# The first query and key rows in four-token packets: one transfer per head pair, 64x64 transposes, order of issue fitted anew

## The chip, the cores and the metric

The kernel runs on one core of one Trainium2 chip. The metric is device microseconds of one execution, as the median of three runs: 359.04 before the change (358.71 to 359.33). One execution was recorded by the hardware profiler; all views of the profile come from it. The engines are TensorE (PE for its products, PEld for its weight loads), VectorE (DVE), ScalarE (ACT), GpSimd (POOL) and SyncE (SP). SP and ACT issue transfers on hardware queues; POOL issues the transfers that also convert from float32 to bfloat16, on a software queue. All queues share 16 DMA engines.

## The reference

The reference has two stages. The first is attention in a sliding window with sinks: each query sees the first four keys and the 128 last ones up to itself. Its output, 3072 tokens of 512 numbers, goes into a mixture of four experts, all of them used for every token and weighted by normalized probabilities.

```python
# q, k, v: (4, 8, 768, 64); n_sink 4, window 128
scores = np.matmul(q, k.transpose(0, 1, 3, 2)) / np.sqrt(D)
keep = (pos[None, :] < n_sink) | ((rel >= 0) & (rel < window))   # rel = query - key position
scores = np.where(keep, scores, -1e9)
a = softmax(scores)                      # in the reference by exp, sum and division
x = (a @ v).transpose(0, 2, 1, 3).reshape(3072, 512)

p = domain_probs / domain_probs.sum(-1, keepdims=True)           # (3072, 4)
out = 0                                  # w1: (4, 512, 1024), w2: (4, 1024, 512)
for e in range(4):
    out += p[:, e:e + 1] * (np.maximum(x @ w1[e], 0) @ w2[e])
```

## The kernel before

The tokens of a batch (768) are worked in three groups of 256, `g` = 0, 1, 2; the 8 heads in four pairs, `hp` = 0 to 3. Two heads of 64 numbers fill the 128 partitions. For each group of a batch, attention needs query and key with the head's numbers on the partitions (tile `qkT`). In batch 0 they are turned by TensorE (`transposes`, tile `tr`); in the later batches by transposing transfers. Then come, pair by pair, the score products (`scores`, tile `sps`), the exponential on ScalarE (tile `aT`), a product with the mask on VectorE, the value products (`values`, tile `od`; a column of ones in `vx` gives the sum of the softmax), the division on VectorE or ScalarE (tile `onat`), and the turn into `xT`, which the experts read. In group 0 of batch 0 the mask is a bias that TensorE adds to the scores (`low`, with the identity as the stationary operand), so nothing is multiplied there.

The experts' first layer (`emit_first`, tile `hps`, line 1106) is a plain product for the first groups. Later it is done by seven products in place of eight on quarters of the matrices (`emit_fast`, tile `cps`, line 1189), whose operands VectorE forms from weights and tokens (`weight_form1`, `tokens`). The second layer is plain for two groups (`emit_second`, line 1433) and by seven products after that (`emit_product`, line 1358).

The first query and key rows, 256 tokens of 8 heads, are loaded as float32 by `load_first`, before anything else: queries on SP's queue, keys on ACT's, in two transfers each, one for heads 0 to 3 and one for heads 4 to 7. A partition holds two neighbouring tokens of each head, 512 bytes at a stretch. `cast_first` converts each half to bfloat16, queries on VectorE and keys on ScalarE. Then four transposes of 128x128 turn a head pair (line 595): two token phases for queries, two for keys, both heads at once. The copy to `qkT` puts the tokens back into their order. The rows of groups 1 and 2 are loaded by POOL with the conversion on the way (`load_nat`), and turned as 128x64 pieces (line 598).

The order of all instructions is made while the program is built. A loop at the end of the kernel keeps an estimated clock for each engine and for the transfers (the dictionary `t`, the functions `pe`, `act`, `dve`, `pool`, `lands`), asks which steps are ready (`options`, `firsts`, `product_ready`, `second_ready`), and emits the best by a rank. Work for VectorE and ScalarE is put on a list with a due time (`later`) and emitted in the order of these (`flush`). The named constants at the head of the kernel are ranks, due times, waiting times and shares of this planner. They do not change what is computed, but what stands before what on each engine; on the chip each engine then takes its instructions strictly in that order. While nothing is ready in the first 20 us of the plan, the loop emits products on zeros (`idle_products`, line 574), whose results nobody reads. Nine of them with 512 columns stand at the very start.

Of the kernel before, what the change touches and what calls it, by code (L numbers as in the profile page):

```python
# [16 lines left out]
def kernel(  # L17
# [42 lines left out]
    NGATE = 5  # L60
    START = {0: (1, 0), 1: (0, 1), 2: (0, 0), 3: (0, 0)}
# [3 lines left out]
    SHARE_OF = (0.634, 1.111, 1.102)  # L65
    LEAD = (1.272, 0.235)
    DUE = 0
    LOW_PRODUCT = 2.791
    LOW_SECOND = 4.402
    HIGH_PRODUCT = 0.207  # L70
    EARLY = 0.154
    GATE = 8921
    GATE0 = 5401
    FORM = 20576
    FORM2 = 37391
    TOKEN00 = 33179
    TOKEN0 = 1119
    WAIT2 = 16164
    WAIT1 = 5898
    LATE3 = 3  # L80
    TOKEN = 11155
    MARGIN = 494
    FULL = 7
    STEP0 = 0.141
    READY = 46
    WIDE = 2
    OPEN = 1.198
# [6 lines left out]
    GROW = 24662  # L94
    ONLY2 = 1
    BEHIND = 7198
# [14 lines left out]
    FLIP = 421  # L111
# [175 lines left out]
    def load_first():  # L287

        raw = {name: mo.tile([P, 2, 4, 2 * D], FP32, name=f"{name}raw", tag=f"wide{i}", bufs=1) for i, name in enumerate("qk")}
        for half in range(2):  # L290
            hs = slice(4 * half, 4 * half + 4)
            for name, src in (("q", q), ("k", k)):
                x = raw[name][:, half]
                (nc.sync if name == "q" else nc.scalar).dma_start(
                    out=x, in_=src[0, hs, 0:G, :].rearrange("h (p t) d -> p h (t d)", t=2),
                )
                nat[0, half, name, "raw"] = x
            landed["first", half] = ((4870.0, 5180.0), (7550.0, 7350.0))[half]
            t["sp"] += 530
# [4 lines left out]
    first = {name: sb.tile([P, 2, H, D], BF16, name="qkn", tag="qkn", bufs=NQB) for name in "qk"}  # L304
# [3 lines left out]
    def cast_first(half):  # L308
        hs = slice(4 * half, 4 * half + 4)

        def cast(at):
            cast_at[half] = at

        part = join(2, cast)
        for i, name in enumerate("qk"):
            def run(engine, i=i, name=name):
                copy(
                    engine, first[name][:, :, hs, :],
                    nat[0, half, name, "raw"].rearrange("p h (t d) -> p t h d", t=2),
                )  # L320
                part(clock(engine, 512))
            later(("dve", "act")[i], landed["first", half][i], 0, run)
# [215 lines left out]
    low = [lent[:, 5 * P:8 * P], lent[:, 8 * P:10 * P]]  # L538
# [1066 lines left out]
```

## Time and profile before

| What | Before |
|---|---|
| Median of 3 runs | 359.04 us (358.71 to 359.33) |
| The profiled execution | 358.95 us, of which its span is 357.2 us |
| TensorE products | 348.8 us busy, 98% of the span |
| VectorE | 306.7 us, 86% |
| ScalarE | 168.7 us, 47% |
| GpSimd | 70.5 us, 20% |
| First transfers of q and k issued | from 0.81 us |
| First product, on zeros | at 1.40 us |
| First transposes of group 0 and of group 1 | at 5.83 and 13.00 us |
| First product of an expert | at 15.10 us |

The span goes from the first to the last recorded instruction; the execution's own time is 1.75 us longer than its span. A group of instructions is named by the line, the engine, the operation, and what it writes and reads. A product counts as busy from its first column to the modelled end of its results, so neighbouring products overlap, and the distance from one start to the next is what a product takes away from the next one: 0.11 us for 256 columns and 0.43 us for the 512 columns of the first products. A DMA is shown by its issue on the issuing engine and by the time from there to its landing. The granted clock of TensorE is 1.00 in all slices.

### The profile page before, as it was taken

The numbers are of one execution on the slowest core, as the hardware profiler recorded it, in microseconds if no ns is written. First come the engines' busy times: TensorE is split into PE (matmuls) and PEld (weight loads), VectorE is DVE, ScalarE is ACT, GpSimd is POOL, SyncE is SP. The second block draws the span as 40 slices with busy tenths as digits, with TensorE's granted clock in tenths as the row PEclk, the third lists the DMA queues.
The fourth block names the chain that finished last, engine by engine and source line by source line (L and its number), as shares of the span: only waits on it lengthen the run. The fifth ranks groups of instructions, "written<-read, shape, count | busy, mean of one in ns | idle before, by whom it ended". The sixth has DMA issues, their size and how long they took to land.

```text
span 357.2 us, 11108 instructions
## 1 busy us (share of the span) xinstructions
PE 348.8 (98%) x4673; PEld 302.6 (85%) x4673; DVE 306.7 (86%) x701; ACT 168.7 (47%) x432; POOL 70.5 (20%) x90
## 2 busy tenths in 40 slices
PE   8999999999999999999999999999999999999995
PEld 3675687777688998998998998899899999999884
DVE  6669999998799899899699799699799699999630
ACT  5866451437882922566444722926443632322110
POOL 8934114311260440420030620000000000000000
PEclk9999999999999999999999999999999999999999
DMA  9999999999993999691086999124112221100011
GB/s 175 185 195 203 230 210 174 137 135 139 227 148 42 138 168 157 75 119 46 32 68 111 148 156 139 50 54 55 44 32 63 59 52 51 37 31 31 1 61 60
DMA packets 115318, 37.86 MB, mean 106 GB/s; under 512 B 97196, under 2 KB 110764, under 8 KB 115268
## 3 DMA queue, kind: packets, MB, share of 16 engines
q0 software_dynamic: 74416, 17.31, 55.4%
q1 hardware_dynamic: 39796, 19.32, 29.3%
q8 instruction: 36, 0.59, 0.7%
q10 hardware_dynamic: 1056, 0.52, 0.6%
q14 instruction: 14, 0.11, 0.1%
HBM read 41.03 MB, written 6.34 MB: 133 GB/s over the span
## 4 chain that ended last, share of the span: by engine, by line
PE 83%; DVE 6%; ACT 5%; DMA 2%; issue 1%; POOL 1%; DVEq 0%
PE cps L1189 35%; PE acc L1358 31%; PE acc L1433 7%; PE hps L1106 3%; PE sps L706 3%; ACT onat L825 2%; PE od L786 2%; ACT aT L746 2%; DMA vx<-in_v_dram 2%; DVE H L1223 1%; DVE cps L1239 1%; DMA gates<-gate_rows 1%; PE od L779 1%; DVE onat L816 1%; DVE H L1254 1%
## 5 line engine op out<-in xcount | busy, mean ns | idle before, releaser
L1189 PEld LDWEIGHTS <-w 128*128 128x128 bf16 x1408 | 87.1, 98 | 3.5 <-issue 1.0
L1358 PEld LDWEIGHTS <-H 128*128 128x128 bf16 x720 | 66.6, 98 | 7.9 <-issue 1.2
L1223 DVE SCALAR_TENSOR_TENSOR H<-cps,gates 128x512 bf16<-128x512 f32 x105 | 69.8, 683 | 0.0
L1358 PE MATMUL acc<-w,H 128*128 128x256 bf16 x432 | 56.8, 273 | 0.1
L1189 PE MATMUL cps<-xT,w 128*128 128x128 bf16 x704 | 52.5, 219 | 0.5 <-ACT onat L825 0.5
L1189 PE MATMUL cps<-T,w 128*128 128x128 bf16 x704 | 52.5, 219 | 0.1
L746 ACT ACTIVATE aT<-sps 128x512 bf16<-128x512 f32 (+1 forms) x96 | 46.5, 571 | 9.7 <-PE sps L706 9.5
L1232 ACT COPY cps<-cps 128x512 f32<-128x512 f32 x44 | 25.7, 592 | 44.2 <-PE cps L1189 33.8
L1405 ACT COPY osb<-acc 128x256 f32<-128x256 f32 x40 | 15.4, 384 | 59.2 <-PE acc L1358 59.2
L825 ACT ACTIVATE onat<-od,R 128x64 bf16<-128x64 f32 x144 | 32.8, 349 | 21.7 <-DVE R L813 21.7
L1358 PE MATMUL acc<-wf,H 128*128 128x256 bf16 x288 | 39.3, 273 | 0.0
L1189 PEld LDWEIGHTS <-qkn 128*128 128x128 bf16 x576 | 34.8, 98 | 1.1 <-issue 0.2
L1239 DVE TENSOR_TENSOR cps<-H,cps 128x512 f32<-128x512 f32 x40 | 27.7, 691 | 9.0 <-PE cps L1189 6.2
L1358 PEld LDWEIGHTS <-S 128*128 128x128 bf16 x320 | 30.2, 98 | 4.2 <-issue 1.0
L1245 ACT COPY H<-cps 128x512 f32<-128x512 f32 x40 | 23.7, 600 | 18.1 <-PE cps L1189 18.1
L1433 PE MATMUL acc<-w,H 128*128 128x512 bf16 x128 | 30.1, 379 | 0.0
L1189 PEld LDWEIGHTS <-vf 128*128 128x128 bf16 x480 | 28.8, 98 | 0.1
L331 POOL DMA_DIRECT2D vx<-in_v_dram x24 | 21.4, 909 | 37.4 <-PE od L786 25.9
L1254 DVE TENSOR_TENSOR H<-H,cps 128x512 f32<-128x512 f32 x40 | 27.0, 680 | 1.7 <-PE cps L1189 1.6
L271 POOL DMA_DIRECT2D rows<-in_q_dram x18 | 16.0, 887 | 61.1 <-DMA qkT<-rows 51.0
L1189 PE MATMUL cps<-T,qkn 128*128 128x128 bf16 x384 | 27.3, 219 | 0.1
L727 DVE TENSOR_TENSOR aT<-aT,mask 128x1024 bf16<-128x1024 bf16 (+1 forms) x36 | 22.8, 641 | 1.9 <-ACT aT L746 1.6
(123 smaller groups left out, 524.2 us busy)
## 6 DMA issues: line engine op xcount, KB each, us to landing
w<-in_moe_w_dram POOLq DMA_DIRECT2D x7, 1024.0 KB, 23.1
out_dram<-osb SPq DMA_DIRECT2D x23, 256.0 KB
gates<-gate_rows SPq DMA_DIRECT2D x40, 128.0 KB
vx<-in_v_dram POOLq DMA_DIRECT2D x24, 128.0 KB, 10.0
rows<-in_q_dram POOLq DMA_DIRECT2D x18, 128.0 KB, 6.4
rows<-in_k_dram POOLq DMA_DIRECT2D x18, 128.0 KB, 6.7
w<-in_moe_w_dram POOLq DMA_DIRECT2D x4, 256.0 KB, 8.4
kraw<-in_k_dram ACTq DMA_DIRECT2D x2, 256.0 KB
```

Source lines behind the costliest of these rows:

```text
L331: nc.gpsimd.dma_start(out=vx[tb][:, :, 0:D], in_=v[b, :, tb * P:(tb + 1) * P, :].rearrange("h p d -> p h d"),)
L727: nc.vector.tensor_mul(x, x, m[:, None, :].to_broadcast([P, n, 2 * w // n]))
L746: nc.scalar.activation(out=a[:, ph], in_=sps[ph][:, 0:w], func=AF.Exp, scale=scale)
L825: nc.scalar.mul(o[:, qi, hp, ph * D:(ph + 1) * D], od[:, qi, ph, 0:D], R[:, qi, ph])
L1189: nc.tensor.matmul(y[:, f], lhsT=A[:, d, f * P:(f + 1) * P], rhs=T[:, d], start=(m in ("P1", "P5") and f == 0 and d == 0), stop=(d == 1), ...
L1223: nc.vector.scalar_tensor_tensor(out=dst, in0=src, scalar=0.0, in1=gate, op0=ALU.max, op1=ALU.mult)
L1232: nc.scalar.copy(out=tiles["Y"], in_=y)
L1239: nc.vector.tensor_add(tiles["V"], c5, tiles["X"])
L1245: nc.scalar.copy(out=c5, in_=y)
L1254: nc.vector.tensor_add(c5, c5, y)
L1358: nc.tensor.matmul(x, lhsT=self.operand(b, g, e, m)[:, f], rhs=forms[e][m][:, f], start=(k == 0 and f == 0 and m in (("P1", "P5", "P2") if ...
L1433: nc.tensor.matmul(op, lhsT=H[:, fb // QF, fb % QF, s], rhs=w2_sb[e][:, fb, :], start=(fb == 0), stop=(fb == NFB - 1),)
```

## The change

The first query and key rows are loaded in another layout. There are now eight transfers, one per head pair for queries and one for keys. Head `a` of a pair takes 64 partitions, and each partition holds four neighbouring tokens of one head, 1024 bytes at a stretch. All queries and the keys of the last pair are on SP's queue, the keys of the first three pairs on ACT's. The conversion follows per pair: the first pair's both on VectorE, later ones queries on VectorE and keys on ScalarE.

A pair is then turned by sixteen transposes of 64x64 instead of four of 128x128: for queries and keys, four token phases for each head, where a head reads and writes its own 64 partitions. The copies to `qkT` put four phases back in order instead of two.

The second bias tile, which nothing read but the second mask, is gone from ScalarE; the second mask is made by two instructions of VectorE from the running maximum (`own`). The clearing of small tiles and the making of the masks are now put on VectorE's list with due times, so that they stand behind the conversion of the second pair's queries and ahead of the third's. Nine idle products with 512 columns at the start become five. Most constants of the planner have new values. In the resulting order VectorE converts the first pair and the second pair's queries, makes the small tiles and the masks, converts the third pair's queries, and only then copies the first turned pair; TensorE turns three pairs, scores three pairs, turns the fourth, and takes the values of two pairs, then of the third, then scores the fourth pair. Seventeen idle products with 256 columns stand in the order instead of twelve. POOL issues the key rows of group 2 before the products for the sink keys and values instead of behind them. From group 1 on, the order on all engines is the old one up to places where neighbours are swapped, in about seven stretches on TensorE and a dozen on VectorE.

```diff
@@ -58,42 +58,49 @@
     NGATE = 5
+    RUN = 4
+    FIRST = (3350.0, 4050.0, 4750.0, 5450.0)
+    CAST = (("dve", "dve"), ("dve", "act"), ("dve", "act"), ("dve", "act"))
+    BEGIN = (3450.0, 3600.0)
+    CLEAR = 1000
+    NACT = 3
+    NIDLE = 5
...
-    SHARE_OF = (0.634, 1.111, 1.102)
-    LEAD = (1.272, 0.235)
+    SHARE_OF = (0.61, 1.111, 1.102)
+    LEAD = (1.272, 0.328)
...
-    GATE = 8921
-    GATE0 = 5401
-    FORM = 20576
-    FORM2 = 37391
-    TOKEN00 = 33179
+    GATE = 9087
+    GATE0 = 5108
+    FORM = 22227
+    FORM2 = 45355
+    TOKEN00 = 35179
...
-    FLIP = 421
+    FLIP = 80
...
@@ -286,40 +293,35 @@
 
     def load_first():
 
-        raw = {name: mo.tile([P, 2, 4, 2 * D], FP32, name=f"{name}raw", tag=f"wide{i}", bufs=1) for i, name in enumerate("qk")}
-        for half in range(2):
-            hs = slice(4 * half, 4 * half + 4)
+        raw = {name: mo.tile([P, NHP, RUN * D], FP32, name=f"{name}raw", tag=f"wide{i}", bufs=1) for i, name in enumerate("qk")}
+        for hp in range(NHP):
             for name, src in (("q", q), ("k", k)):
-                x = raw[name][:, half]
-                (nc.sync if name == "q" else nc.scalar).dma_start(
-                    out=x, in_=src[0, hs, 0:G, :].rearrange("h (p t) d -> p h (t d)", t=2),
+                x = raw[name][:, hp]
+                (nc.scalar if name == "k" and hp < NACT else nc.sync).dma_start(
+                    out=x,
+                    in_=src[0, 2 * hp:2 * hp + 2, 0:G, :].rearrange("h (p t) d -> h p (t d)", t=RUN),
                 )
-                nat[0, half, name, "raw"] = x
-            landed["first", half] = ((4870.0, 5180.0), (7550.0, 7350.0))[half]
+                nat[0, hp, name, "raw"] = x
             t["sp"] += 530
 
     def copy(engine, out, in_):
         (nc.scalar.copy if engine == "act" else nc.vector.tensor_copy)(out=out, in_=in_)
 
-    first = {name: sb.tile([P, 2, H, D], BF16, name="qkn", tag="qkn", bufs=NQB) for name in "qk"}
+    first = {name: sb.tile([P, NHP, RUN, D], BF16, name="qkn", tag="qkn", bufs=NQB) for name in "qk"}
     qkn_free[-2:] = [1e12] * 2
     cast_at = {}
 
-    def cast_first(half):
-        hs = slice(4 * half, 4 * half + 4)
+    def cast_first(hp):
 
         def cast(at):
-            cast_at[half] = at
+            cast_at[hp] = at
 
         part = join(2, cast)
         for i, name in enumerate("qk"):
-            def run(engine, i=i, name=name):
-                copy(
-                    engine, first[name][:, :, hs, :],
-                    nat[0, half, name, "raw"].rearrange("p h (t d) -> p t h d", t=2),
-                )
-                part(clock(engine, 512))
-            later(("dve", "act")[i], landed["first", half][i], 0, run)
+            def run(engine, name=name):
+                copy(engine, first[name][:, hp].rearrange("p t d -> p (t d)"), nat[0, hp, name, "raw"])
+                part(clock(engine, 256))
+            later(CAST[hp][i], FIRST[hp], 100 * hp, run)
 
     def rows_at(b, g):
         return max(landed.get(("qk", b, tb), 1e12) for tb in (2 * g, 2 * g + 1))
@@ -535,36 +537,40 @@
     nc.vector.tensor_tensor_scan(own, ident, ident, 0.0, ALU.add, ALU.max)
     two = own[:, None, :].to_broadcast([P, 2, P])
     LOW = 32768.0
-    low = [lent[:, 5 * P:8 * P], lent[:, 8 * P:10 * P]]
+    low = lent[:, 5 * P:8 * P]
     nc.vector.tensor_scalar(
-        out=low[0].rearrange("p (n q) -> p n q", n=3)[:, 0::2], in0=two, scalar1=LOW, scalar2=-LOW, op0=ALU.mult, op1=ALU.add,
+        out=low.rearrange("p (n q) -> p n q", n=3)[:, 0::2], in0=two, scalar1=LOW, scalar2=-LOW, op0=ALU.mult, op1=ALU.add,
     )
-    nc.vector.tensor_scalar(out=low[0][:, P:2 * P], in0=own, scalar1=-LOW, scalar2=None, op0=ALU.mult)
-    nc.vector.memset(low[0][0:NSINK, 0:2 * P], 0.0)
-    nc.scalar.activation(out=low[1][:, 0:P], in_=own, func=AF.Copy, scale=-LOW)
-    nc.scalar.activation(out=low[1][:, P:2 * P], in_=own, func=AF.Copy, scale=LOW, bias=-LOW)
+    nc.vector.tensor_scalar(out=low[:, P:2 * P], in0=own, scalar1=-LOW, scalar2=None, op0=ALU.mult)
+    nc.vector.memset(low[0:NSINK, 0:2 * P], 0.0)
     mask0 = consts.tile([P, 3 * P], BF16, name="mask0")
     mask1 = consts.tile([P, 2 * P], BF16, name="mask1")
-    t["dve"] = t["act"] = 4600.0
-    cast_first(0)
-    flush(4700.0)
     for x in vx:
         nc.vector.memset(x[:, :, D:DX], 1.0)
-    t["dve"] += 240.0
 
     vsd = {}
     half = consts.tile([P, 2], BF16, name="half")
     ksd = [consts.tile([P, NHP, 32], BF16, name=f"ksd{i}") for i in range(2)]
-
-    nc.vector.memset(half, 0.0)
-    for ph in range(2):
-        nc.vector.memset(half[64 * ph:64 * ph + 64, ph:ph + 1], 1.0)
-    for x in ksd:
-        nc.vector.memset(x, 0.0)
-    for x, y in zip((mask0, mask1), low):
-        nc.vector.tensor_scalar(out=x, in0=y, scalar1=1 / LOW, scalar2=1.0, op0=ALU.mult, op1=ALU.add)
-    t["dve"] += 400.0
-    cast_first(1)
+    t["dve"], t["act"] = BEGIN
+    for hp in range(NHP):
+        cast_first(hp)
+
+    def clear(engine):
+        nc.vector.memset(half, 0.0)
+        for ph in range(2):
+            nc.vector.memset(half[64 * ph:64 * ph + 64, ph:ph + 1], 1.0)
+        for x in ksd:
+            nc.vector.memset(x, 0.0)
+        t["dve"] += 400.0
+
+    def masks(engine):
+        nc.vector.tensor_scalar(out=mask0, in0=low, scalar1=1 / LOW, scalar2=1.0, op0=ALU.mult, op1=ALU.add)
+        nc.vector.tensor_scalar(out=mask1[:, 0:P], in0=own, scalar1=-1.0, scalar2=1.0, op0=ALU.mult, op1=ALU.add)
+        nc.vector.tensor_copy(out=mask1[:, P:2 * P], in_=own)
+        t["dve"] += 500.0
+
+    later("dve", 3600.0, CLEAR, clear)
+    later("dve", 3600.0, CLEAR + 300, masks)
 
     acc = [psum.tile([P, 2 * G], FP32, name=f"acc{i}", tag=f"o{i}", bufs=1) for i in range(2)]
 
@@ -582,7 +588,7 @@
 
         if b not in qkT:
             qkT[b] = sb.tile([P, 2, NHP, S], BF16, name="qkT", tag="qkT", bufs=1)
-        ready = max(cast_at[hp // 2] if (b, g) == (0, 0) else rows_at(b, g), free_at(2 if (b, g) == (0, 0) else 1))
+        ready = max(cast_at[hp] if (b, g) == (0, 0) else rows_at(b, g), free_at(2 if (b, g) == (0, 0) else 1))
         slots, trs = [], []
         for i in range(2 if (b, g) == (0, 0) else 1):
             slots.append(pick())
@@ -590,15 +596,19 @@
             ring[slots[i]] = 1e12
         hs = slice(2 * hp, 2 * hp + 2)
         for i in range(2):
+            if (b, g) == (0, 0):
+                x = trs[i][:, i].rearrange("c t p -> c (t p)").rearrange("c (t p) -> c t p", t=RUN)
+                for tt in range(RUN):
+                    for ph in range(2):
+                        pr = slice(64 * ph, 64 * ph + 64)
+                        nc.tensor.transpose(x[pr, tt], first["qk"[i]][pr, hp, tt], ident[pr, pr])
+                continue
             for tt in range(2):
-                if (b, g) == (0, 0):
-                    nc.tensor.transpose(trs[i][:, i, tt], first["qk"[i]][:, tt, hs], ident)
-                    continue
                 for ph in range(2):
                     nc.tensor.transpose(
                         trs[0][64 * ph:64 * ph + 64, i, tt], nat[b, 2 * g + i][:, 2 * hp + ph, tt * D:(tt + 1) * D], ident,
                     )
-        done = pe(4 * P, ready, n=4, switch=0 if (b, g) == (0, 0) else 2)
+        done = pe(4 * P, ready, n=4, switch=2)
         dst = qkT[b][:, :, hp, g * G:(g + 1) * G]
 
         def copied(at):
@@ -610,7 +620,8 @@
             part = join(2, copied)
             for i, engine in enumerate(("dve", "act")):
                 def run(engine, i=i):
-                    copy(engine, dst[:, i].rearrange("c (p t) -> c p t", t=2), trs[i][:, i].rearrange("c t p -> c p t"))
+                    x = trs[i][:, i].rearrange("c t p -> c (t p)")
+                    copy(engine, dst[:, i].rearrange("c (p t) -> c p t", t=RUN), x.rearrange("c (t p) -> c p t", t=RUN))
                     part(clock(engine, 2 * P))
                 later(engine, done, 0, run)
         else:
@@ -697,7 +708,7 @@
         biased = b == 0 and g < BIASED
         if biased:
             for ph in range(2):
-                nc.tensor.matmul(sps[ph][:, 0:w], lhsT=ident, rhs=low[min(g, 1)], start=True, stop=False, skip_group_check=True)
+                nc.tensor.matmul(sps[ph][:, 0:w], lhsT=ident, rhs=low, start=True, stop=False, skip_group_check=True)
             pe(2 * w, ready, n=2)
         c = 0
         for (kb, qb, nq) in GROUPS[g]:
@@ -887,7 +898,7 @@
 
         def flip_ready(self):
             _, b, g, hp = self.flips[0]
-            rows = cast_at.get(hp // 2, 1e12) if (b, g) == (0, 0) else rows_at(b, g)
+            rows = cast_at.get(hp, 1e12) if (b, g) == (0, 0) else rows_at(b, g)
             return max(rows, free_at(2 if (b, g) == (0, 0) else 1), scored_at.get(b - 1, 0.0))
 
         def options(self):
@@ -1461,7 +1472,7 @@
 
 
 
-    idle_products(acc[1], 9)
+    idle_products(acc[1], NIDLE)
     mix = Mixture()
     att = Attention(0)
     work = [
```

More of the change, by code (lines that the diff above doesn't have):

```diff
@@ L64 @@
     MIX = 4
-    SHARE_OF = (0.634, 1.111, 1.102)
-    LEAD = (1.272, 0.235)
+    SHARE_OF = (0.61, 1.111, 1.102)
+    LEAD = (1.272, 0.328)
     DUE = 0
[L68 to L71, printed above, removed]
-    GATE = 8921
-    GATE0 = 5401
-    FORM = 20576
-    FORM2 = 37391
-    TOKEN00 = 33179
-    TOKEN0 = 1119
-    WAIT2 = 16164
-    WAIT1 = 5898
+    LOW_PRODUCT = 2.872
+    LOW_SECOND = 4.475
+    HIGH_PRODUCT = 0
+    EARLY = 0.207
+    GATE = 9087
[3 more added lines that the diff above has]
+    TOKEN00 = 35179
+    TOKEN0 = 1517
+    WAIT2 = 16819
+    WAIT1 = 5930
     LATE3 = 3
-    TOKEN = 11155
-    MARGIN = 494
+    TOKEN = 12447
+    MARGIN = 154
     FULL = 7
-    STEP0 = 0.141
-    READY = 46
+    STEP0 = 0.15
+    READY = 17
     WIDE = 2
-    OPEN = 1.198
+    OPEN = 0.991
     ONACT = 1
@@ L93 @@
     MASKD = 99999999
-    GROW = 24662
+    GROW = 24255
     ONLY2 = 1
-    BEHIND = 7198
+    BEHIND = 7891
     CHORES = 2
```

## The prediction

> **What bounds the kernel now.** I read the page first, then busy time by stage, then the chain of work of the first 34 us, then the first 20 us of the timeline, and last the DMA's rate and the landing of single loads.
>
> ```profile
> span 357.2 us, 11108 instructions
> ...
> PE 348.8 (98%) x4673; PEld 302.6 (85%) x4673; DVE 306.7 (86%) x701; ACT 168.7 (47%) x432; POOL 70.5 (20%) x90
> ```
>
> TensorE is the bound: 8.4 us of the span without a product. Busy time by stage (columns PE, PEld, DVE, ACT, POOL, clock, DMA, GB/s) shows where they lie:
>
> ```profile
> 5.00:10.00 5.00, 4.56 (x47) 2.57 (x45) 2.32 (x7) 3.88 (x10) 5.00 (x7) 1.00 1.97 193
> 10.00:15.00 5.00, 4.68 (x85) 3.17 (x81) 3.20 (x10) 3.64 (x9) 4.50 (x10) 1.00 1.83 179
> ...
> 20.00:25.00 5.00, 4.15 (x53) 3.41 (x50) 3.58 (x14) 2.54 (x5) 0.51 (x1) 1.00 1.42 199
> 25.00:30.00 5.00, 5.00 (x59) 3.45 (x58) 3.27 (x8) 1.90 (x4) 3.13 (x4) 1.00 1.82 185
> ...
> 340.00:357.00 17.00, 13.45 (x124) 11.81 (x121) 3.62 (x10) 1.86 (x5) 0.00 (x0) 1.00 0.18 63
> ```
>
> From 25 us PE is nearly full; the stretches between 30 and 340 us lose about 1.5 us together (0.86 of it from 100 to 150). So time won at the start shows at the end only if what PE does at 25 us comes earlier. What leads there is the chain (start, length, what):
>
> ```profile
> 3.52 5.80 DMA vx<-in_v_dram
> 9.32 0.04 issue
> 9.36 0.26 PE od L786 x3
> ...
> 12.03 0.55 PE acc L574 x5
> 12.58 0.18 PE od L786 x6
> 12.76 0.03 issue
> 12.79 0.29 PE tx L847 x2
> 13.07 0.57 PE tr L598 x16
> ```
>
> The v rows of block 1 land at 9.32; then come the values of group 0, five idle products, and the transposes of group 1, begun at 13.00. The timeline gives what must be ready:
>
> ```profile
> 1.40 4.59 PE L574 MATMUL acc<-lent 128*128 128x512 bf16 x13 [1.40 <-DVE lent L496]
> ...
> 4.93 0.62 ACT L302 CAST qkn<-kraw 128x512 bf16<-128x512 f32 x1 [1.19 <-DMA kraw<-in_k_dram]
> ...
> 5.83 0.61 PE L595 MATMUL tr<-ident,qkn 128*128 128x128 bf16 x8
> ...
> 6.80 0.34 PE L706 MATMUL sps<-qkT 64*128 64x256 bf16 x4
> ...
> 7.55 1.25 ACT L746 ACTIVATE aT<-sps 128x384 bf16<-128x384 f32 x3
> ```
>
> Issue plus time to landing, load by load: k rows of group 1, 5.38+6.7=12.1 (used 13.00); w1 of expert 0 in quarters, 7.11+7.5=14.6 (15.10), 8.73+8.0=16.7 (17.34), 9.48+8.9=18.4 (18.93), 10.21+9.3=19.5 (20.15); its w2, 24.9 (26.49). PE is only 0.5 to 0.6 us behind the weights, 0.9 behind the rows. The DMA's rate (last column) as it starts and runs:
>
> ```profile
> 2.80:3.00 0.20, 0.20 (x2) 0.01 (x1) 0.12 (x2) 0.20 (x1) 0.20 (x1) 1.00 0.71 207
> ...
> 3.40:3.60 0.20, 0.20 (x2) 0.09 (x1) 0.12 (x2) 0.20 (x2) 0.20 (x2) 1.00 1.15 348
> ...
> 6.20:6.40 0.20, 0.20 (x7) 0.19 (x5) 0.20 (x1) 0.15 (x1) 0.20 (x2) 1.00 2.28 167
> ```
>
> Added over its steps: 262 KB are moved by 3.4, 524 KB by 4.16, the first 1049 KB by about 6.0; only 135 KB of them before 3.0, at 54 to 207 GB/s.
>
> **First rows.** The same 1049 KB go as 8 transfers of 131 KB in 1024 packets of 1 KB, not 4 in 2048 of 512 B. Lower bound of the gain: none, if bytes set the rate. Upper: if the ramp before 3.0 is bound by packets, twice its 135 KB pass, and 135 KB at 343 GB/s are 0.39 us. Two more bounds agree: 512 KB (of source) of 512 B packets took 1.7 us between two landings (10.4 to 12.1), of 1 KB packets 1.1 to 1.7 (the quarters). I take 0.3, and the same for everything queued behind. A fall in rate below today's would need late issues: SP issues at 0.47 each, so the fifth begins at 2.7; with the 1.3 us that lie between 0.81 and the first bytes it starts at 4.0, before the stream could want it (about 4.9). No loss there.
>
> **VectorE.** Its constants are done at 3.36 (memsets of vx). First pair: 262 KB at 3.4 less some of the ramp, plus 0.3 to 0.8 from last byte to cast (524 KB at 4.16; casts at 4.48 and 4.93): 4.0. Casts of 128x256 at half of the 0.43 to 0.57 row, 0.28 each: q0 and k0 to 4.56. Pair 1 lands at 4.7, q1 to 5.0. This wait holds what is queued behind: the clears (0.45, 3.30 to 3.75 in the trace) and masks (0.71 before, one instruction more, 0.75) to 6.2, q2 to 6.5, then the first copy of a turned pair (0.38) to 6.9. So the first score products wait for this copy until 6.9, against 6.80 today: casting earlier wins nothing for pair 0. What is won is that three pairs are scored in a row.
>
> **ScalarE.** One more issue (0.55) pushes its table load to 2.5-3.7; two activations (0.31 and 0.29) go. The k3 cast (landing 6.2 to 6.6) and two copies (0.3 apart) end at 7.3 to 7.6; exponentials begin there (7.55 today). Six of 128x384 at 0.40 apart (1.25 for three less the 0.46 tail) end at 9.8 to 10.0.
>
> **TensorE.** Off: four cold 512-column products (0.43 each, 1.7 us of filler) and 16 transposes of 128x128. On: 64 of 64x64. Sixteen of 128x64 took 0.64, eight of 128x128 0.61 (0.31 for a pair), so a pair costs 0 to 0.33 more; PE waits for casts then, and the wait hides it. If it did not, the fourth pair's is on the path, 0.3. Idle 256-column products go from 12 to 17, 0.11 each. Values of pairs 0 and 1 follow the v landing at 9.0 (9.32 less 0.3) and the exponentials; the third comes at 9.9 to 10.1; its normalization and turn at 10.9 to 11.3 (1.05 after the product, as 10.47 to 11.5 today); seven idle products, 0.77; the last values, 0.2. The transposes of group 1 begin at 12.05 to 12.4, after their rows (11.8 to 12.1). I take 12.2: **0.8 us** before today's 13.00.
>
> The clock: cold products stood 0.43 apart from 1.40 to 5.22, and 256-column ones went from 0.21 to about 0.11 only near 5.5, after 4.0 us without a gap. Now the unbroken run ends at 1.40 + 5x0.43 + 4x0.21 = 4.4, and PE then waits for casts, in between two pairs' transposes, until 6.5. By the rows alone I can't tell whether the fast rate comes at 5.5 all the same; the sum takes it so, since PE has work in most of that time, and a rival has the other case.
>
> [...]
>
> **Carried on?** With 0.8 off, the weights are asked for at 14.3, 16.5, 18.1, 19.4 and w2 at 25.7; less 0.3 they land at 14.3, 16.4, 18.1, 19.2 and 24.6. It just fits; with no gain in the stream about 0.3 of the 0.8 is lost at the first quarter. Order is otherwise kept: hps, values, then group 1 in the same sequence.
>
> **Queues.** SP issues three more (1.4 us) ahead of the probabilities, the eight sink loads (last at 7.96, now 9.4) and the second probabilities (9.4): used at 13.92 and 22.63, so free. POOL issues the k rows of group 2 (0.94) before the sink keys and values: these move to 14.2-15.9, used at 16.19 and 18.21, free; those rows, used at 29.19 after 27.8, come sooner.
>
> **Refit.** Beyond 13 us the PE order differs in some seven places out of a thousand rows, DVE in about a dozen, SP in none; no work is added. Bounds: the 1.5 us PE loses there could all go, or as much be added. I take 0, since the same sort of work only changes places with its neighbour.
>
> **Sum.** The profiled execution is 358.95 (span 357.2 and 1.75 around it), 0.09 under the median 359.04. 358.95 - 0.8 + 0 = 358.15, so **358.2**.
>
> **Rivals.**
> *The gain is eaten* (0.22): the stream is no faster and the DVE queue runs late. With pair 0 at 4.4 and the other steps kept, the first copy ends at 7.3, the six exponentials at 10.6, group 1 begins at 12.85: 358.8; with the quarters' 0.3 lost too, 359.1. For it: PE is only 0.5 us behind the weights.
> *PE stays slow* (0.10), the one to slower. If the fast rate comes only after the third score group, each group takes 1.4 for 0.7, the third's exponentials end at 12.1 for 10.0, group 1 begins near 14.2: 360.1. It decides if the slow rate lasts past 8 us. Against it: the transposes are work too.
> *The new order stalls* (0.15): a product in front of its operand in the DVE-full stretch (DVE 19.9 of 20 us from 60 to 80) costs 1 to 2 us: 359.2 to 360.2, past today from 0.8 us on.
>
> **Numbers.** The forecast has 0.53, its own range 357.4 to 358.7. About 0.2% (0.7 us) is what a measurement of this kernel tells from no change: below 358.3 is faster, above 359.8 slower. Of the forecast 0.45 is faster; so are 0.03 of the eaten gain (a faster order behind it) and 0.03 of the third rival (a stall of the old order gone with the new one): 0.51. Slower: 0.10 for the clock, 0.12 stalls, 0.02 eaten: 0.24. The rest, 0.25, is the same. The range 357.3 to 360.1 leaves out a tenth on each side.
>
> **What would show it.** Right: first rows moved by 5.7; six exponentials of 128x384 in a row from about 7.5; transposes of group 1 at 12.2; the first quarter's products at 14.3; w2's at 25.7; all later work 0.8 sooner. Wrong: 256-column products 0.21 apart past 6 us (clock); PE waiting on w at 14 to 20 us (stream); PE short of full between 50 and 340 us by over 2 us (order).

## The result and the profile after

| | Before | After |
|---|---|---|
| Median | 358.92 us (358.71 to 359.33, 4 runs) | 387.46 us (387.31 to 387.91, 4 runs) |
| Ratio | | 1.0798 (95% interval 1.0783 to 1.0813) |
| The profiled execution | 358.95 us, span 357.2 | 387.47 us, span 385.7 |
| Transposes of group 1 begin | 13.00 us | 41.58 us |

The change costs 28.5 us. The forecast was 358.2, with a range from 357.3 to 360.1: the sign is wrong and the time lies far outside. The head of the page of after:

```profile
span 385.7 us, 11205 instructions
...
PE 351.6 (91%) x4713; PEld 304.2 (79%) x4722; DVE 306.4 (79%) x706; ACT 167.9 (44%) x430; POOL 68.6 (18%) x90
```

TensorE is busy for 2.8 us more, but stands 34.1 us without a product where it was 8.4. Busy time by stage of after (columns as in the prediction: PE, PEld, DVE, ACT, POOL, clock, DMA share, GB/s):

```profile
3.20:3.60 0.40, 0.40 (x3) 0.12 (x2) 0.15 (x5) 0.00 (x0) 0.40 (x2) 1.00 0.13 46
3.60:4.00 0.40, 0.40 (x4) 0.28 (x3) 0.00 (x0) 0.00 (x0) 0.40 (x1) 1.00 0.14 49
5.00:10.00 5.00, 0.00 (x0) 0.00 (x0) 0.00 (x0) 0.56 (x1) 4.43 (x6) 1.00 1.55 162
10.00:15.00 5.00, 0.63 (x16) 0.50 (x16) 0.49 (x2) 0.10 (x1) 0.00 (x0) 1.00 1.66 187
15.00:20.00 5.00, 0.96 (x17) 0.60 (x17) 0.92 (x9) 0.30 (x1) 0.75 (x1) 1.00 0.52 86
20.00:25.00 5.00, 0.44 (x16) 0.44 (x16) 0.79 (x3) 0.68 (x2) 0.74 (x1) 1.00 0.35 60
25.00:30.00 5.00, 1.82 (x15) 0.45 (x11) 0.80 (x3) 0.00 (x0) 0.89 (x1) 1.00 0.54 77
30.00:35.00 5.00, 0.56 (x3) 0.13 (x4) 0.00 (x0) 1.29 (x5) 0.88 (x1) 1.00 1.24 199
35.00:40.00 5.00, 5.00 (x54) 2.84 (x52) 2.15 (x7) 2.77 (x8) 2.91 (x7) 1.00 1.24 131
```

From 5 to 35 us PE is busy for 4.4 of 30 us, and the loss lies there. Group 1 is 28.58 us late at 41.58, and the execution is 28.5 us longer. The work behind it is as fast as before: PE is busy for 288.73 of the 290 us from 50 to 340 before, and for 288.18 of the 290 us from 78.5 to 368.5 after.

The first two lines name the cause. While only the first rows are on the way, the share of the DMA engines is 0.13 where before it was 1.15, and 46 GB/s move where there were 348. Two engines of 16 would be 0.125; since the share adds up the time of packets and passes 1 in before, this is a first reading, which experiment one tests. The timeline of after shows what came of it (start, length, engine, line; in brackets the idle time ahead and what ended it):

```profile
0.81 3.44 ACTq L300 DMA_DIRECT2D kraw<-in_k_dram  x3
0.81 13.53 SPq L300 DMA_DIRECT2D qraw<-in_q_dram  x4
...
11.36 0.29 DVE L308 CAST qkn<-qraw 128x256 bf16<-128x256 f32 x1 [8.00 <-DMA qraw<-in_q_dram]
...
14.38 5.84 SPq L300 DMA_DIRECT2D kraw<-in_k_dram  x1
14.90 0.40 ACT L308 CAST qkn<-kraw 128x256 bf16<-128x256 f32 x1 [9.34 <-DMA kraw<-in_k_dram]
18.34 0.29 DVE L308 CAST qkn<-qraw 128x256 bf16<-128x256 f32 x1 [6.48 <-DMA qraw<-in_q_dram]
...
33.71 0.41 ACT L308 CAST qkn<-kraw 128x256 bf16<-128x256 f32 x1 [11.14 <-DMA kraw<-in_k_dram]
...
34.44 0.48 PE L711 MATMUL sps<-lent,ident 128*128 128x384 bf16 x1 [7.62 <-ACT qkT L308]
...
41.58 0.64 PE L608 MATMUL tr<-ident,qkn 128*64 128x128 bf16 x16
```

The first pair is converted (cast) at 11.36, the last keys at 33.71; the second score group of PE waits 7.62 us for a copy that stands behind that last conversion on ScalarE, and from there PE works without a long pause up to group 1. SP's two issues took 1.00 us together before; its first four now take 13.53, and the fifth 5.84. So everything queued behind them is late too. The chain of after, its first 42 us (start, length, what):

```profile
2.32 5.10 SPq L300
...
7.46 6.88 SPq L300
...
14.38 5.84 SPq L300
...
20.26 13.73 DMA scratch<-in_moe_domain_probs_dram
...
34.02 4.55 DMA vsf<-in_v_dram
...
38.69 1.06 POOL vsd L656
39.75 1.74 POOL vx L333 x2
```

The probabilities, issued at 1.86 before, are issued at 20.26; the sink values follow, POOL waits for these (its last 0.70 us before 38.69), and the next loads of v and of weights stand behind POOL. So two chains reach 41.5 us together: the one over the last keys' conversion, and this one.

The pattern of the load differs in its outermost step. It runs over heads first (2), then over runs of tokens (64), then over 256 numbers; the load before ran over 128 runs of tokens first. An estimate from the share: 0.13 of 16 engines are 2.1, so two engines work on such a load, as many as it has heads outermost, and the same two on all of them, since the share is 0.13 with loads on both queues.

### The profile page after: what moved, and what is told of

Its sections match the earlier page's. It is cut to its first block, busy times and chain, and to the rows that moved or that the text cites. A ratio compares the mean times of both kernels' runs of the same rounds, so it can differ in the third digit from the quotient of the medians.

```text
span 385.7 us, 11205 instructions
## 1 busy us (share of the span) xinstructions
PE 351.6 (91%) x4713; PEld 304.2 (79%) x4722; DVE 306.4 (79%) x706; ACT 167.9 (44%) x430; POOL 68.6 (18%) x90
## 4 chain that ended last, share of the span: by engine, by line
PE 78%; DMA 10%; SPq 5%; ACT 3%; DVE 2%; POOL 1%; issue 1%; DVEq 0%; POOLq 0%
PE cps L1200 35%; PE acc L1369 30%; PE acc L1444 7%; SPq L300 5%; DMA w<-in_moe_w_dram 4%; DMA scratch<-in_moe_domain_probs_dram 4%; PE sps L717 2%; PE hps L1117 2%; PE od L797 2%; ACT onat L836 2%; DMA xT<-onat 1%; DMA vsf<-in_v_dram 1%; PE od L790 1%; ACT aT L757 1%; POOL vx L333 0%
## 5 line engine op out<-in xcount | busy, mean ns | idle before, releaser
L1444 PE MATMUL acc<-w,H 128*128 128x512 bf16 x119 | 29.0, 379 | 0.6 <-issue 0.2
L738 DVE TENSOR_TENSOR aT<-aT,mask 128x1024 bf16<-128x1024 bf16 (+1 forms) x36 | 22.7, 637 | 2.2 <-ACT aT L757 2.2
```

What stands on the lines that cost most here:

```text
L738: nc.vector.tensor_mul(x, x, m[:, None, :].to_broadcast([P, n, 2 * w // n]))
L1444: nc.tensor.matmul(op, lhsT=H[:, fb // QF, fb % QF, s], rhs=w2_sb[e][:, fb, :], start=(fb == 0), stop=(fb == NFB - 1),)
```

## The experiments

Theory A: the spread over the engines explains the loss. Rivals: the refitted order, the gap in TensorE's work (the clock), the number of packets or of issues, and the smaller transposes.

**One: the loads alone.** A kernel that leaves out the computation issues loads of 131 KB on SP's queue with 2, 4, 8, 16 heads outermost, then of one head in 128 runs, the same bytes in packets of 512 B, and as two loads of 64 partitions; then six loads of two heads in a row and six of 128 runs.

> Loads alone, the whole computation left out (the output is filled from a scratch tile). One after another, each waited for: 131 KB in 1 KB packets into 128 partitions from 2, 4, 8 and 16 heads (twice), from 128 runs of one head, the same bytes in 512 B packets, and as two transfers of 64 partitions. Then six two-head loads issued without a wait between, then six of 128 runs. Theory 1: moving time in proportion to 1/heads; at the 23 GB/s that one engine had in the changed kernel, 2.8 us for 2 heads, 1.4 for 4, 0.7 for 8, 0.35 for 16, beside a fixed part of about 2 us; 128 runs as 16 heads; six two-head loads 17 us, with issues on SP that grow to about 3 us each; six of 128 runs about 2.5 us of moving. Theory 2: all 1 KB loads alike, 512 B ones faster.

Timeline of that kernel (a copy on VectorE waits for each load):

```profile
7.20 0.29 DVE L39 COPY heads<-heads 128x256 f32<-128x256 f32 x1 [5.49 <-DMA heads<-in_q_dram]
11.56 0.29 DVE L39 COPY heads<-heads 128x256 f32<-128x256 f32 x1 [4.06 <-DMA heads<-in_q_dram]
14.90 0.29 DVE L39 COPY heads<-heads 128x256 f32<-128x256 f32 x1 [3.04 <-DMA heads<-in_q_dram]
17.76 0.29 DVE L39 COPY heads<-heads 128x256 f32<-128x256 f32 x1 [2.57 <-DMA heads<-in_q_dram]
...
51.12 10.91 SPq L59 DMA_DIRECT2D many<-in_q_dram  x6
70.16 0.96 DVE L61 COPY lots<-many 128x1536 f32<-128x1536 f32 x1 [19.07 <-DMA many<-in_q_dram]
71.14 2.70 SPq L63 DMA_DIRECT2D lots<-in_q_dram  x6
75.58 0.29 DVE L64 COPY last<-lots 128x256 f32<-128x256 f32 x1 [4.46 <-DMA lots<-in_q_dram]
```

The same bytes take 5.5, 4.1, 3.0 and 2.6 us with 2, 4, 8 and 16 heads outermost, and 2.1 with 128 runs, whether in packets of 1 KB or of 512 B. Above these 2.1 us the loads by heads take 3.4, 2.0, 0.9 and 0.5 more, about half as much for each doubling of the heads. Split into two loads of 64 partitions the bytes take 2.8 to 3.1. Six loads of two heads take 19.07 us, six of 128 runs 4.46. In the long row 48 GB/s move at a share of 0.13 (from 54 to 68 us), as in after: more loads in flight do not help, as they would if each took engines of its own. And the issuing engine is held: six issues last 10.91 us in place of 2.70.

**Two: the same layout, 64 runs of tokens outermost.** Only the loads differ from after. In one kernel each of the eight loads brings one head of two pairs, so that 64 runs of tokens are outermost; in the other each head has a load of its own (16 of 66 KB).

```diff
-                (nc.scalar if name == "k" and hp < NACT else nc.sync).dma_start(
-                    out=x,
-                    in_=src[0, 2 * hp:2 * hp + 2, 0:G, :].rearrange("h (p t) d -> h p (t d)", t=RUN),
+                (nc.scalar if name == "k" and i < NACT else nc.sync).dma_start(
+                    out=raw[name][64 * ph:64 * ph + 64, 2 * half:2 * half + 2],
+                    in_=src[0, 4 * half + ph:4 * half + 4:2, 0:G, :].rearrange("h (p t) d -> p h (t d)", t=RUN),
```

> The changed kernel, with its eight first transfers cut another way: each takes one head of two neighbouring pairs (64 partitions, two heads' packets behind each other on a partition) instead of both heads of one pair. Count (8), bytes (131 KB each), packet size (1 KB), queues, layout in the tile, transposes and planner constants are the same; only the outermost step of the DRAM pattern is now 64 token runs, not 2 heads. Theory 1 (the transfer is dealt out to DMA engines along its outermost step, so two heads use 2 of 16 engines): first rows moved by about 6 us at over 300 GB/s, transposes of group 1 at 12 to 13 us, total 357.5 to 360. Theory 2 (packets of 1 KB, or twice as many transfers, are slow on the hardware queues): no change, 386 to 388. Theory 3 (the clock or the refitted order costs the time): no change in what follows the loads, over 380.

> The changed kernel with sixteen first transfers, one per head (64 partitions, 66 KB), in the order of the pairs. Theory 1: total 357.5 to 360 as in the run above, the first pair's casts earlier (about 4 us) than there, the issues of SP (10) longer by some 2.4 us. Theory 2 in its form that the number of transfers costs: slower than the changed kernel, over 390; in its form that the packets cost: 386 to 388.

Two pairs to a load: 364.72 us, ratio 1.0165 (1.0151 to 1.0179). From 3.2 to 3.6 us 218 GB/s move there at a share of 1.22, where after has 46 at 0.13. So 22.7 of the 28.5 us go with the outermost step alone; theory A holds for most of the loss, though both kernels were forecast at 357.5 to 360, and 5.7 us are left. One head to a load: 367.58, 1.0239 (1.0225 to 1.0253): there ten issues of about 0.7 stand in a row on SP; the first pair's queries are cast at 4.25, the third's only at 9.34, the fourth's at 12.28 and its keys at 13.47.

**Three: the refit alone.** Before, with the 22 planner constants of after and nothing else.

> The kernel before with the changed kernel's values for the 22 planner constants that both have (shares, due times, waits and ranks); loads, casts, transposes and idle products as before. It measures the refit alone. Theory 1 and 2 both: within 1.5 us of the kernel before (357.5 to 360.5), since the stretches after 13 us are nearly the same. Theory 3: most of the 28.5 us, over 370.

358.72 against 359.07 us, ratio 0.9995 (0.9986 to 1.0004): nothing, as forecast.

**Four: the clock.** The 5.7 us left in experiment two had slow products in them. In its timeline two products of 384 columns take 0.82 us together; in before they take 0.49. This is the slow rate of the prediction, at which neighbouring products stand about twice as far apart, 0.21 us for 0.11 with 256 columns (before first, then experiment two):

```profile
6.38 0.49 PE L700 MATMUL sps<-lent,ident 128*128 128x384 bf16 x2
...
10.72 0.82 PE L711 MATMUL sps<-lent,ident 128*128 128x384 bf16 x2
11.91 0.82 PE L711 MATMUL sps<-lent,ident 128*128 128x384 bf16 x2
13.10 0.82 PE L711 MATMUL sps<-lent,ident 128*128 128x384 bf16 x2
```

Two kernels test it, and a pair in experiment five: that of experiment two with eleven more idle products of 512 columns at the start; and before with five idle products in place of nine.

```diff
     idle_products(acc[1], NIDLE)
+    for _ in range(11):
+        nc.tensor.matmul(acc[1], lhsT=zeros[:, 0:P], rhs=zeros, start=True, stop=True)
```

> The run with one head of two pairs per transfer (364.7, 5.7 above the kernel before), with eleven more products on zeros at the very start, which the planner's clock does not count, so that the order behind them is the same and TensorE is busy until about 7.2 us, when the first pair is converted. Theory A (what is left of the loss is mostly the slow TensorE rate: 384-column products stood 0.41 apart until 15 us there): score products at the fast rate from about 10 us, the transposes of group 1 at 14.5 to 16 instead of 18.1, total 360.5 to 362.5. Theory B (it is mostly that the first rows land later, the hardware queues being served slower once the software queue's loads run beside them): within 1 us of 364.7.

> The kernel before with five instead of nine 512-column products on zeros at the start, the planner's clock counting nine, so that the order behind is the same. TensorE then waits from 4.4 us until its first transposes at 5.8. Loads, casts and layout are those of before, so only the clock can differ. Theory A: the slow rate lasts some 3 us longer or more, group 1 starts 0.5 to 2 us later, total 359.5 to 361. Theory B: no change, 358.5 to 359.5.

With eleven more the first two of those pairs take 0.50, the third 0.82 again; the time is 362.64 us, 1.0099 (1.0082 to 1.0115), 2.1 less. The slow rate is not all gone: group 1 begins at 17.76, for 18.12 without the products and 14.5 to 16 forecast, and of the six times three are 361.9 to 362.2 and three, the profiled one among them, 363.1 to 363.4. Before with five has 359.45, 1.0014 (0.9999 to 1.003), on the border of the two theories. Of its twelve times eight are 358.7 to 359.7 and four 360.5 to 361.2, and the profiled one reached the fast rate by 6 us. The slow rate has a price, 2.1 us with these eleven products; whether the four long times of before with five are due to it is not shown.

**Five: the order of after with loads over 128 partitions.** One load per pair again, but two tokens of a head per packet, 128 runs outermost, and the transposes of 128x128: all other parts of the change stay. Then the same with four more idle products of 512 columns, and with these but without the twelve idle products of 256 columns that follow after 9 us of the plan.

```diff
-                    in_=src[0, 2 * hp:2 * hp + 2, 0:G, :].rearrange("h (p t) d -> h p (t d)", t=RUN),
+                    in_=src[0, 2 * hp:2 * hp + 2, 0:G, :].rearrange("h (p t) d -> p h (t d)", t=2),
...
-                for tt in range(RUN):
-                    for ph in range(2):
-                        pr = slice(64 * ph, 64 * ph + 64)
-                        nc.tensor.transpose(x[pr, tt], first["qk"[i]][pr, hp, tt], ident[pr, pr])
+                for tt in range(2):
+                    nc.tensor.transpose(trs[i][:, i, tt], first["qk"[i]][:, tt, hs], ident)
```

> The changed kernel with its transfers still one per head pair over all partitions, but two tokens per packet (512 B) with the token runs as outermost step of both patterns, and the four 128x128 transposes of before: everything of the change but the four-token layout. With the loads on 16 engines and 131 KB per issue of 0.45 us, the queues should be fed as fast as before. Theory A (late rows are cured, clock still slow because TensorE waits from 4.4 us): 359.5 to 362. Theory B (landing alone matters): 357.5 to 359.3. If eight transfers as such are the cost: over 363.

> The same with four more products on zeros at the start, as many as the kernel before has (busy to about 5.7 us). Theory A: faster than the run without them by 0.5 us or more, 357.5 to 359. Theory B: the same as the run without them, within 0.4.

> The best run so far (one transfer per head pair, 512 B packets, 128x128 transposes, nine products on zeros at the start), without the twelve 256-column products on zeros that the loop put in from 9 us of its plan on; the planner's clock still counts them, so nothing else moves. If these products are what held group 1 at 12.94, where 12.1 to 12.4 was predicted: transposes of group 1 at 12.2 to 12.5, total 358.2 to 358.7. If the chain of exponentials and turns holds it, or the w1 quarters' landings hold what comes after: the same total as with them, 359.0 to 359.3. If TensorE falls back to its slow rate in the gaps: over 359.5.

They take 360.27 us, 1.0040 (1.0026 to 1.0054); 359.11, 1.0004 (0.9994 to 1.0015); and 358.90, 0.9997 (0.998 to 1.0014). The first keeps the five idle products of the change. It reaches the fast rate, waits 1.15 us for a conversion, and has slow products again from 9.33 on (the granted clock is 0.50 from 9 to 12 us):

```profile
7.03 0.42 PE L601 MATMUL tr<-ident,qkn 128*128 128x128 bf16 x4 [1.15 <-DVE qkn L308]
...
9.33 0.82 PE L707 MATMUL sps<-lent,ident 128*128 128x384 bf16 x2
...
14.66 0.64 PE L605 MATMUL tr<-ident,qkn 128*64 128x128 bf16 x16
```

Four more idle products take 1.2 us off. The second kernel shows what the new order does when its loads are in time and the rate is fast:

```profile
3.76 0.77 DVE L308 CAST qkn<-qraw 128x256 bf16<-128x256 f32 x1 [0.40 <-DMA qraw<-in_q_dram]
...
7.38 0.40 ACT L308 CAST qkn<-kraw 128x256 bf16<-128x256 f32 x1 [0.17 <-DMA kraw<-in_k_dram]
...
8.22 2.41 ACT L753 ACTIVATE aT<-sps 128x384 bf16<-128x384 f32 x6
...
10.53 0.48 PE L793 MATMUL od<-vx,aT 128*128 128x65 bf16 x6
...
12.94 0.53 PE L605 MATMUL tr<-ident,qkn 128*64 128x128 bf16 x12
```

Six exponentials stand in a row, as forecast, but from 8.22 and not 7.3 to 7.6: the last keys are cast at 7.38, and two copies behind them on ScalarE come before the exponentials. Group 1 begins at 12.94, not 12.2. The idle products are not what holds it: without them it is 12.93, and PE waits for the last pair's exponentials instead.

**Six: can a start that is a little earlier be seen at all?** Before without six idle products of 256 columns.

```diff
-            idle_products(acc[1], 1, G)
+            (idle_products(acc[1], 1, G) if now < 9000 else pe(G))
```

> The kernel before without the six 256-column products on zeros after 9 us of the plan (five of them lie at 11.87, ahead of the last values of group 0), the planner's clock counting them. If they hold group 1: transposes at 12.5 in place of 13.0 and total 358.3 to 358.8; if the rows (landing at 12.1) or later loads hold it: 358.8 to 359.3.

Group 1 at 12.70, the first product of an expert at 14.80, its second layer at 26.18, each 0.3 earlier; the time 359.08, 0.9997 (0.9981 to 1.0012). The interval leaves room for a gain of 0.3 us, but shows none.

**Seven: what is left of the four-token layout.** 3.6 us stay in experiment four. Four loads of 262 KB, all heads of one parity each, with the eleven products, test whether the number of issues matters; the next kernel lets the keys' queue begin with the other half of the partitions; the third does that with eight loads and four more idle products.

> The four-token layout with its 64x64 transposes, loaded by four transfers of 64 partitions and 262 KB (all even heads, all odd heads, of q and of k) in place of eight of 131 KB, with the eleven more products at the start. In the eight-transfer form the first quarter of w1 landed at 16.1 us, against 14.6 before. If the issues of 0.6 to 0.7 us each starve the hardware queues there: all first rows by 6.5 us, the quarter at 14.4 to 14.9, total 359 to 361. If transfers into 64 partitions are slow as such: the quarter at 15.5 or later, total 362 or more.

> The four 262 KB loads of e10_four, but the keys' queue begins with the upper 64 partitions while the queries' queue begins with the lower, so both halves of the partitions are written at every moment; nothing else differs. Theory H, that each half of the partitions has a limit of its own of about 200 GB/s: 300 GB/s and more between 3.2 and 6 us where e10_four had 200, first casts at 6.0 to 6.6 in place of 8.5, transposes of group 1 at 14.3 to 15.0 in place of 16.8, time about 361.2 (two us below 363.3). Theory P, that a packet pattern of two or four heads on 64 partitions is slow whichever half it goes to: 200 GB/s again, 363.3 within 0.4.

> The eight loads of e1_parity, with the keys' halves in the opposite order to the queries', and four more cold products of 512 columns (nine in all, as the kernel before had). Theory H: the loads of the first two pairs move at over 300 GB/s, first cast at 4.5 to 5.0 in place of 6.7, third and fourth pair's casts at 6.5 to 7.5 in place of 9.0 to 10.1, no cold products after 7 us, group 1 at 13.0 to 13.5, time 358.7 to 359.5. Theory P: casts as in e1_parity, time at least 362.5.

Four loads: 363.26 us, 1.0112 (1.0086 to 1.0138); crossed 363.60, 1.0126 (1.0095 to 1.0157); eight, crossed, 363.88, 1.0127 (1.0107 to 1.0146). Theory P came true twice: neither fewer issues nor another order of the halves helps. Windows of before, then of the four loads:

```profile
4.00:4.40 0.40, 0.40 (x3) 0.12 (x2) 0.40 (x1) 0.00 (x0) 0.40 (x1) 1.00 1.15 342
...
4.00:4.40 0.40, 0.40 (x3) 0.12 (x2) 0.00 (x0) 0.00 (x0) 0.40 (x2) 1.00 1.15 202
4.80:5.20 0.40, 0.40 (x2) 0.14 (x1) 0.00 (x0) 0.00 (x0) 0.40 (x1) 1.00 1.09 189
```

The engines are as busy as in before (1.15), but 202 GB/s move where before had 342. With the halves crossed it is 202 to 207 from 4.4 to 5.6 us.

**Eight: what makes these loads slow.** Loads alone once more, the computation left out. The first kernel puts 1049 KB on SP's queue in eight forms of 131 KB, the second on two queues with the halves equal or crossed, the third takes the pattern apart.

> Loads alone (the computation is left out, the output is not the reference's): eight loads of 131 KB in a row on SP's queue, no software queue beside them, all with an outermost step of 64 or 128 token runs; six forms, each twice. full1k: 128 partitions, one packet of 1 KB each; lower1k and upper1k: two packets of 1 KB into each of the lower or upper 64 partitions; turns1k: the same by turns into lower and upper; full512: 128 partitions, two packets of 512 B; lower512: four packets of 512 B into the lower 64. Theory A, that 64 partitions are slow as such: full1k and full512 at about 300 GB/s (1049 KB in 3.5 us, as six of 131 KB moved in 4.46 with issue and latency), lower1k, upper1k and turns1k at about 200 GB/s, 5.2 us. Theory B, that they are slow only beside the software queue's transfers: all 1 KB forms within a tenth of each other. Theory C, that each half has its own limit: lower1k and upper1k slow, turns1k like full1k.

> Loads alone (the computation is left out, the output is not the reference's): 1049 KB on two queues, SP's and ACT's, no software queue beside them, each form twice. same: four loads of 262 KB into 64 partitions, both queues in the lower half, then both in the upper; crossed: the two queues always in opposite halves; lower: all four in the lower half; full: eight loads of 131 KB over 128 partitions. Theory H: crossed and full used 4.5 to 5.5 us after the first issue (2.1 of latency and 1049 KB at 300 GB/s and more), same and lower 6.7 to 7.5 (1049 KB at 200). Theory P: same, crossed and lower within 0.4 of each other, above full.

> Loads alone (the computation is left out, the output is not the reference's), as in e15_halves: four loads of 262 KB, two on SP's queue and two on ACT's, each form twice. lower: 64 lower partitions, four packets of 1 KB each (7.4 to 7.9 us from first issue to use in e15_halves). spread: the same packets on every second of the 128 partitions. two: 128 partitions, two packets of 1 KB. thin: 64 lower partitions, eight packets of 512 B. narrow: 32 partitions for each queue, eight packets of 1 KB. halfk: 128 partitions, four packets of 512 B, the kernel before's form. Theory H2, that what counts is how far the partitions of one load lie spread: spread, two and halfk 5.5 to 6.3 us, lower, thin and narrow 7.4 to 8. Theory N, that the number of partitions of one load counts: two and halfk 5.5 to 6.3, lower, spread and thin 7.4 to 8, narrow 10 and more. Theory S, that the packet's size or the number of heads in one pattern counts: lower, spread and narrow alike at 7.4 to 8, thin and halfk alike.

On one queue 1049 KB take 6.1 to 6.6 us over 128 partitions and 7.4 to 8.0 in either half or by turns; an issue takes 0.46 to 0.50 over 128 and 0.64 to 0.69 over 64. Eight issues alone last 3.7 to 4.0 us and 5.1 to 5.5, so one queue can't tell slow issues from slow transfers. On two queues the issues are over within 1.9 us, and the times remain: both in the same half 7.5 and 7.8, crossed 7.4 and 7.6, all in the lower half 7.8 and 7.9, over 128 partitions 6.2. So theory H is out. The timeline of the third kernel, its first round:

```profile
14.21 2.29 DVE L42 COPY spread<-lower 128x4096 f32<-128x4096 f32 x1 [8.16 <-DMA lower<-in_k_dram]
22.20 2.29 DVE L42 COPY two<-spread 128x4096 f32<-128x4096 f32 x1 [5.70 <-DMA spread<-in_k_dram]
30.21 2.29 DVE L42 COPY thin<-two 128x4096 f32<-128x4096 f32 x1 [5.72 <-DMA two<-in_k_dram]
40.43 2.29 DVE L42 COPY narrow<-thin 128x4096 f32<-128x4096 f32 x1 [7.92 <-DMA thin<-in_k_dram]
50.05 2.29 DVE L42 COPY halfk<-narrow 128x4096 f32<-128x4096 f32 x1 [7.33 <-DMA narrow<-in_k_dram]
58.45 2.29 DVE L42 COPY lower<-halfk 128x4096 f32<-128x4096 f32 x1 [6.11 <-DMA halfk<-in_k_dram]
```

Each line's wait belongs to the form named in its bracket. 64 neighbouring partitions take 8.16 us with packets of 1 KB and 7.92 with 512 B, 32 partitions for each queue 7.33. The same packets on every second of 128 partitions take 5.70, two packets of 1 KB on all 128 take 5.72, four of 512 B take 6.11. The second round has 7.8, 8.2 and 7.2 for the first three, and 5.9 and 5.1 for the next two; of the last form it waits for one part only. In the windows, 64 neighbours move 205 GB/s at a share of 1.14 (10 to 11 us), the same packets on every second partition 380 at 1.08 (20 to 21 us). So theory H2 fits: in these forms what counts is how far one load spreads over the partitions, not their number, the size of the packet or the number of heads. What slows a load into neighbouring partitions, and why crossing the halves on two queues brought nothing, is not shown by these runs. The four-token layout has each head on 64 neighbouring partitions, so each load tried in the kernel with runs of tokens outermost falls into one half. A load with the runs of tokens outermost and both halves inside was not tried.

## Why the prediction was wrong, point by point

- **First rows** is the step that failed. It gave the stream 0.3 us of gain, with "none, if bytes set the rate" as its worse bound, and said of a loss that it "would need late issues". It bounded a price by bytes and packets, and the price was set by a third thing that no row of before contains: the outermost step of the load's pattern. Measured: 46 to 49 GB/s at first in place of 348, the last cast at 33.71 in place of about 7, 28.6 us at group 1. Late issues came as well, as a result: up to 6.88 us for one, not 0.47. With the share of after, taken as two engines of 16, a row shown gives an estimate: 348 GB/s at a share of 1.15 are 38 GB/s for a share of 2/16, or 44 for 2/16 of the rate, and 1049 KB take 24 to 28 us.
- None of the rivals had this. By the estimate just worked out, the sum would have come out about 20 us slower.
- **VectorE, ScalarE, TensorE**: with loads in time and nine idle products (second kernel of experiment five) the first casts came as forecast (3.76 and 4.45; 4.0 and about 4.3), six exponentials in a row too. But the last keys were cast at 7.38, for a landing forecast at 6.2 to 6.6, and the exponentials began 0.6 to 0.9 later than forecast. Of the 0.8 us at group 1, 0.06 was there. This comes nearest to the rival that the gain is eaten (358.8 to 359.1; measured 359.11).
- **The clock** was a rival with a chance of 0.10, priced at 1.9 us; the sum took the fast rate. It could not be the main thing in after, since PE had nothing to do. But the first kernel of experiment five, which has the change's five idle products and its loads in time, is that rival: slow products again at 9.33, group 1 at 14.66 (the rival said 14.2), 360.27 us (360.1). So with the loads mended, though with the old transposes, this term of the sum failed as well. Four idle products more are worth 1.2 us there, eleven more 2.1 in experiment four.
- **Queues** were called free, with issues of 0.47 each. With issues of 5 to 7 us they were not: the probabilities moved from 1.86 to 20.26 and onto the chain.
- **Refit** at 0 was right, as far as the constants go when put into before (0.9995). That the work behind the start is unchanged was right too, and that its delay carries to the end: 28.58 at group 1, 28.5 in the time. That a gain of 0.3 us carries as well is not shown (experiment six).
- **64x64 transposes** were right as priced: sixteen took 0.63 in after and 0.44 at the fast rate (with the four loads of experiment seven), for 0.31 forecast at best and 0.64 at worst.
- **Sum of the causes**: the 28.5 us are about 22.7 for the two heads outermost (experiment two) + 2.1 for the slow rate (four) + 3.6 left; these are medians taken at different times and add up to 28.4. For the 3.6, slow loads into 64 partitions (202 GB/s for 342) are the shown cause of late casts. That they make up all of it is argued from experiment five, where nothing is left with 128 partitions, but also with other transposes; some of the slow rate is left in it too, in the profiled execution at least.

## What to carry to other kernels

Before a load is rearranged, write down its pattern on both sides and look at the outermost step: in experiment one it decided how fast the same bytes moved (5.5 us with 2 heads, 2.1 with 128 runs), and two heads outermost cost 22.7 us here with not a byte more. Then look at which partitions it writes: 64 neighbours moved 202 GB/s where 128 moved 342. A new layout's effect on transfers is no term to be bounded by bytes and packets alone, when no transfer of that shape stands in the trace.

## What the hardware showed beyond that

- Several loads with two heads outermost held the issuing engine: one issue took 5.10 to 6.88 us in after, and six in a row 10.91 alone, where six of 128 runs took 2.70. So everything that the same queue issued later was late too: in after the probabilities, at 20.26 in place of 1.86.
- By an estimate, 48 GB/s alone would have moved the 1049 KB by about 25 us (21.9 us, from about 3 us on); the last cast was at 33.71. From 4.4 us on POOL's loads ran beside them; that they slowed the rows is the author's estimate, not tested.
- The clock column reads 1.00 over the first 50 us of after and of before. Yet idle products of 512 columns stood 0.43 apart at the start of both, four times the 0.11 of 256 columns later on for twice the columns, and two products of 384 columns took 0.82 at 35.28 in after. In the kernel of experiment two the column reads 0.50 from 8 to 9 us, in the first of experiment five from 9 to 12. The distance between equal products is the surer reading.
